# A masked row maximum taken head by head on VectorE, in a fused attention and token/channel mixer

## The chip, the cores and the metric

The kernel runs on one core of a Trainium2 chip. The metric is the device time of one execution in microseconds (us). TensorE is called PE in the profile (PEld are its weight loads), VectorE is DVE, ScalarE is ACT, GpSimd is POOL, and SyncE, which only issues DMAs here, is SP.

## The reference

Windowed attention over 8 batches, 8 heads, 576 positions of 64 values (the window is the position itself and the 63 before it), and behind it two mixers on the result x (576 tokens of 512 channels per batch):

```python
scores = scale * np.matmul(q, k.transpose(0, 1, 3, 2))
mask = (rel >= 0) & (rel < window)
scores = np.where(mask, scores, -1000000000.0)
scores = scores - np.max(scores, axis=-1, keepdims=True)
attn = np.exp(scores)
attn = attn / (np.sum(attn, axis=-1, keepdims=True) + 1e-09)
x = np.matmul(attn, v)                      # then heads side by side: B, S, H * D
xt = x.transpose(0, 2, 1)
h = np.maximum(xt @ w_tok1, 0.0) @ w_tok2   # token mixer, 576 -> 256 -> 576
u = x + h.transpose(0, 2, 1)
h2 = np.maximum(u @ w_ch1, 0.0) @ w_ch2     # channel mixer, 512 -> 1536 -> 512
return u + h2
```

The four mixer weights arrive as 64-bit floats. The kernel turns them into fp32 itself and splits each into a high and a low part, since each large product is made of three matmuls of rounded parts.

## The kernel before, in words

**Tiles.** The 72 blocks of 64 queries are done as 36 tiles, i = 0 to 35. A tile holds two query blocks on the 128 partitions and all 8 heads; its scores lie in two PSUM banks, `s[u]` with u = 0 and 1, four heads of 128 keys each. Nine tiles make a pair of batches (`TPP = 9`).

**One round of the loop.** For tile i the loop transposes the exponentials (`pt_transpose`, PE, then a copy by ACT), multiplies with v (`av`), scales by the reciprocal sums (`recip`, `norm`, on DVE) and splits x (ACT high part, POOL low part, `split_x`) for the token mixer. In the same round the softmax of tile i+1 runs: `softmax(i+1, u)` on DVE makes the masked scores and the negative row maximum `nm`, `softmax_exp` on ACT makes the exponentials head by head with their sums. At its end PE makes the scores of tile i+2 (`qk`). PE fills what is left with `tok1` (L387) and pieces of `tok2` (L428, L435).

**The mask.** For the first N_PE = 7 tiles PE adds the mask by a matmul (L287), and DVE takes the maximum straight from PSUM (L309) and scales it (L310). From tile 7 on, DVE does it in two instructions over all four heads of a bank: L312 reads the scores from PSUM, multiplies by the scale, adds the mask and writes `e` to SBUF; L315 reads `e` and takes the maximum of each head.

**The weights.** `job_load` loads a piece of 64-bit weights (`raw`), `job_convert_a` (L204, L206, L207) and `job_convert_b` (L216, L218, L219) convert it on DVE, POOL adds the halves (L221), and `job_finish` splits it (ACT high part; POOL or DVE low part). The table `JOBS` says in which rounds a conversion stands: one in rounds -1 to 5 and 12, and later in six of nine rounds.

**Order.** The order of the work on each engine is the order in which the code is written; nothing is rescheduled. All loads are issued by SP in that order. Round 0's loads are written out by hand ahead of the loop, those of the first batch's keys in five pieces.

**After the attention.** From 262 us on the kernel does the channel mixer, which PE fills almost alone; the change does not touch it.

Of the kernel before, what the change touches and what calls it, by code (L numbers as in the profile page):

```python
# [10 lines left out]
F32 = mybir.dt.float32  # L11
# [4 lines left out]
AF = mybir.ActivationFunctionType  # L16
ALU = mybir.AluOpType
AX = mybir.AxisListType
PSUM = bass.MemoryType.PSUM

B, H, S, D = 8, 8, 576, 64
C = H * D
P = 128
BLK = 64
NBLK = S // BLK
NPAIR = B // 2
TPP = 9
NT = NPAIR * TPP
# [11 lines left out]
N_FIRST = 28  # L40


JOBS = {i: 1 if i < 6 or i == 12 or i > 6 and i % TPP not in (0, 3, 5) else 0 for i in range(-1, 37)}
PIECES = {22: (1, 0), 23: (1, 0), 31: (1, 0), 32: (1, 0), 33: (1, 0), 34: (1, 0), 35: (3, 0), 36: (2, 1)}

TOK1_FROM, TOK1_SLOW, TOK2_FROM = 2, 4, 7
# [1 line left out]
N_PE, N_EARLY = 7, 4  # L48
# [9 lines left out]

HOME = {"m1": "c2", "m6": "c3", "m7": "c4", "m5": "c5", "m2": "c6", "m4": "c0", "m3": "c1"}
SLOT, NSLOT = NPROD * 2 * P, 3  # L60
NEG = -1.0e9

NEG_PE = -2.0 ** 33

F64_LOW = 2.0 ** -15
F64_HIGH = struct.unpack("<f", struct.pack("<I", 0x47EFFFFF))[0]
# [7 lines left out]
def tile_blocks(i):  # L74

    p, t = divmod(i, TPP)
    if t == 4:
        return (2 * p, 8), (2 * p + 1, 8)
    b, t = (2 * p, t) if t < 4 else (2 * p + 1, t - 5)
    return (b, t), (b, t + 4)  # L80
# [3 lines left out]
def mixer_kernel(ctx: ExitStack, tc: tile.TileContext, qh, kh, vh, wt1, wt2, wc1, wc2, out):  # L84
    nc = tc.nc
    scale = 1.0 / math.sqrt(D)
# [36 lines left out]
    with ExitStack() as actx:  # L123
        pa = actx.enter_context(tc.tile_pool(name="pa", bufs=1))
        qctx = ExitStack()
        pq = qctx.enter_context(tc.tile_pool(name="pq", bufs=1, side="right"))

        mask = [pa.tile([P, P], F32, name=f"mask{m}") for m in range(2)]

        kbs, loaded, cpool = {}, {}, [pq]  # L130

        def load_k(i):
            p, t = divmod(i, TPP)
            if t in (0, 4):
                b = 2 * p + (t == 4)
                kbs[b] = pq.tile([P, H // 2, (NBLK + 1) * BLK], F32, name=f"k{b}", tag="k", bufs=2)
                if b != 0:
                    nc.sync.dma_start(kbs[b], kh[b])

# [10 lines left out]
        maskr = [pa.tile([P, P], F32R, name=f"maskr{m}") for m in range(2)]  # L150
# [7 lines left out]
        def warm(k):  # L158
            for _ in range(k):
                nc.tensor.matmul(idle, zero[:, :P], zero, start=True, stop=True)  # L160
# [3 lines left out]
        for m in (1, 0):  # L164
            nc.gpsimd.memset(mask[m], 0.0)
            for half in range(2):
                mh = mask[m][half * BLK:(half + 1) * BLK]
                nc.gpsimd.affine_select(out=mh, in_=mh, compare_op=ALU.is_ge, fill=NEG,
                                        base=-1, pattern=[[1, P]], channel_multiplier=-1)
                nc.gpsimd.affine_select(out=mh, in_=mh, compare_op=ALU.is_ge, fill=NEG,  # L170
                                        base=BLK, pattern=[[-1, P]], channel_multiplier=1)
            if m == 1:
                nc.gpsimd.memset(mask[1][0:BLK, 0:BLK], NEG)
            nc.scalar.activation(maskr[m], mask[m], AF.Copy, scale=NEG_PE / NEG)

        for c in range(2):
            nc.gpsimd.tensor_copy(swapped[:, c * BLK:(c + 1) * BLK], ident[:, (1 - c) * BLK:(2 - c) * BLK])
# [53 lines left out]
        def job_load():  # L231
            if to_load:
                n = to_load.pop(0)
                src, _, _, o, m = jobs[n]
                raw = cpool[0].tile([P, CW], I64, name=f"raw{n}", tag="raw", bufs=3)
                nc.sync.dma_start(raw[:, :m], src[:, o:o + m])
                to_convert.append((n, raw))
# [3 lines left out]
        def job_convert_a():  # L241
            if to_convert:
                n, raw = to_convert.pop(0)
                to_convert_b.append((n, to_f32_a(raw, jobs[n][4], n, n >= N_FIRST)))

        def job_convert_b():
            if to_convert_b:
                n, part = to_convert_b.pop(0)
                to_finish.append((n, to_f32_b(*part)))
# [17 lines left out]
        s_ps, e_sb, st = {}, {}, {}  # L267

        def qk(i):

            qt, on_pe = loaded[i][0], i < N_PE
            s = []
            for u in range(2):

                if i == 1:
                    tag, bufs = "h", 2
                elif (i, u) == (N_PE, 1) or 2 <= i < N_PE and (2 * i + u) % 3 == 0:
                    tag, bufs = "up", 1
                else:
                    tag, bufs = "s", 2  # L280
                s.append(ps.tile([P, 4, P], F32, name=f"s{i}_{u}", tag=tag, bufs=bufs))
                s_ps[i, u] = s[u]
                if i == 0 and u == 0:
                    warm(4)
                if on_pe:
                    mk = maskr[1 if tile_blocks(i)[0][1] == 0 else 0]
                    nc.tensor.matmul(s[u], identr, mk.unsqueeze(1).to_broadcast([P, 4, P]), start=True, stop=False,  # L287
                                     skip_group_check=True)
            if i == 0:
                warm(3)  # L290
            for j in range(4):
                for u in range(2):
                    r = slice(u * BLK, (u + 1) * BLK)
                    for half, (b, n) in enumerate(tile_blocks(i)):
                        nc.tensor.matmul(s[u][half * BLK:(half + 1) * BLK, j], qt[r, j, half],
                                         kbs[b][r, j, n * BLK:n * BLK + P],
                                         start=not on_pe, stop=True, skip_group_check=on_pe)

        def softmax(i, u):
            if u == 0:  # L300
                st[i] = (pa.tile([P, H], F32, name=f"nm{i}", tag="nm", bufs=3),
                         pa.tile([P, H], F32, name=f"sum{i}", tag="sum", bufs=3))
            nm, sm = st[i]
            mk = mask[1 if tile_blocks(i)[0][1] == 0 else 0]
            e = pa.tile([P, 4, P], F32, name=f"e{i}_{u}", tag="e", bufs=4)
            e_sb[i, u] = e
            nmu = nm.rearrange("p (j u) -> p j u", u=2)[:, :, u]
            if i < N_PE:
                nc.vector.tensor_reduce(out=nmu, in_=s_ps[i, u], axis=AX.X, op=ALU.max, negate=True)  # L309
                nc.vector.tensor_scalar_mul(nmu, nmu, scale)  # L310
                return
            nc.vector.scalar_tensor_tensor(  # L312
                out=e, in0=s_ps.pop((i, u)), scalar=scale,
                in1=mk.unsqueeze(1).to_broadcast([P, 4, P]), op0=ALU.mult, op1=ALU.add)
            nc.vector.tensor_reduce(out=nmu, in_=e, axis=AX.X, op=ALU.max, negate=True)  # L315

        def softmax_exp(i, u):
            e = e_sb[i, u]
            nm, sm = st[i]
            src, by = (s_ps.pop((i, u)), scale) if i < N_PE else (e, 1.0)  # L320
            for h in range(4):
                g = 2 * h + u
                nc.scalar.activation(e[:, h], src[:, h], AF.Exp, bias=nm[:, g:g + 1], scale=by,  # L323
                                     accum_out=sm[:, g:g + 1])
# [22 lines left out]
        def recip(i):  # L347
            _, sm = st.pop(i)
            ri = pa.tile([P, H], F32, name=f"ri{i}", tag="ri", bufs=2)
            nc.vector.tensor_scalar_add(ri, sm, 1e-9)  # L350
            nc.vector.reciprocal(ri, ri)
            return ri

# [119 lines left out]
        def run_pieces(k):  # L473
            for _ in range(min(k, len(pieces))):
                tok2(*pieces.pop(0))

        load_k(0)
        load_q(0)
        k0, kh0 = (x[:, :, :8 * BLK].rearrange("p j (g n) -> p j g n", g=2) for x in (kbs[0], kh[0]))
        for g in range(2):  # L480
            nc.sync.dma_start(k0[:, :, g, :P], kh0[:, :, g, :P])
        load_q(1)
        for g in range(2):
            nc.sync.dma_start(k0[:, :, g, P:], kh0[:, :, g, P:])
        job_load()
        load_v(0)
        nc.sync.dma_start(kbs[0][:, :, 8 * BLK:], kh[0, :, :, 8 * BLK:])
        load_q(2)
        job_load()
        load_v(1)  # L490
        tok1_plan, n = {}, 0
        for i in range(TOK1_FROM, NT + 1):
            m = min(n + (1 if i < TOK1_SLOW else 2), i)
            tok1_plan[i] = range(n, m)
            n = m
        qk(0)
        for i in range(-1, NT + 1):
            if 0 <= i and i + 2 < NT:
# [5 lines left out]
            store_u()  # L504
            n_jobs = JOBS[i]
            if i == NT - 1:
# [8 lines left out]
                    pts.append(pt_transpose(i, 1))  # L515
            if i + 1 < NT:
                softmax(i + 1, 0)
            if early and i > 0:
                norm(*normed.pop())
            if 0 <= i < NT:  # L520
                ri = recip(i)
# [13 lines left out]
                    job_convert_a()  # L535
            if i == NT - 1:
                pts.append(pt_transpose(i, 1))
            if i + 1 < NT:
                softmax(i + 1, 1)
            if i < N_PE - 1:  # L540
                for _ in range(n_jobs):
# [38 lines left out]
    with ExitStack() as bctx:  # L580
# [105 lines left out]
        u = ul.pop(0)  # L686
# [12 lines left out]
        for ct in range(NCT):  # L699
# [3 lines left out]
            op = new_op("0", ct)  # L703
# [84 lines left out]
        for j in range(1, N_PLAIN):  # L788
            u, last = ul.pop(j), j == N_PLAIN - 1
# [4 lines left out]
            for half in range(2):  # L794
                g = []
# [33 lines left out]
                for ct in range(NCT):  # L829
                    op = new_op(f"{j}_{half}", ct)  # L830
# [141 lines left out]
```

## Time and profile before

| | |
|---|---|
| median of 3 runs | 842.85 us (841.65 to 843.45) |
| the profiled execution's own time | 843.08 us |
| its span, first to last instruction | 841.3 us |
| mean granted TensorE clock | 0.993 |
| PE busy in the span | 820.7 us |
| DVE, ACT, POOL busy in the span | 529.1, 336.6, 104.6 us |
| 57.30 to 249.88 us (tiles 6 to 34): DVE busy | 173.2 of 192.58 us |
| 262 to 841 us: PE busy | 574.2 of 579 us |

The time outside the span is 843.08 - 841.3 = 1.8 us. Rows of the timeline give start, duration, engine, line and operation, and in brackets the idle time ahead and what ended it. Rows on the same engine can overlap by some 0.08 us: the next instruction starts while the last one is leaving the pipeline, so costs are taken from start to start. A row of the chain of waits gives start, length and the work on the chain.

### The profile page before, as it was taken

Reading aid. Unit: us, or ns where it says so; the run is one execution under the profiler, and the core shown is the slowest. Engines: PE = TensorE matmul, PEld = TensorE weight load, DVE = VectorE, ACT = ScalarE, POOL = GpSimd, SP = SyncE. Lnnn points to the kernel's source line nnn. Section 1 sums busy time; section 2 is a strip of 40 time slices with the busy share of each in tenths; the row PEclk is TensorE's granted clock in tenths of the full one; section 3 lists DMA queues with packets and bytes.
Section 4 is the critical chain, followed back from the end, with each engine's and each line's share of the span. In section 5 each row is a group of like instructions: output and inputs, shape, how many; then the busy total and the mean of one; then the engine's idle time right before and its main releaser. Section 6 shows DMA issues by size and latency. Waiting matters only on the chain.

```text
span 841.3 us, 14830 instructions
## 1 busy us (share of the span) xinstructions
PE 820.7 (98%) x5878; PEld 681.4 (81%) x5878; DVE 529.1 (63%) x940; ACT 336.6 (40%) x1017; POOL 104.6 (12%) x110
## 2 busy tenths in 40 slices
PE   8989999999999999999999999999999999999998
PEld 5668888888879878888888888878888878888886
DVE  5889988888884795666425535367635367625252
ACT  6778889888885441213203211024202033202020
POOL 4433434343332000000000000000000000000000
PEclk9999999999999999999999999999999999999999
DMA  9657687677644546744413642324542424542002
GB/s 329 210 202 250 206 253 242 218 246 249 206 134 151 195 121 187 209 139 135 141 73 111 246 194 87 138 88 138 187 188 88 138 91 169 171 170 88 1 1 100
DMA packets 71621, 136.49 MB, mean 162 GB/s; under 512 B 7040, under 2 KB 41856, under 8 KB 69632
## 3 DMA queue, kind: packets, MB, share of 16 engines
q1 hardware_dynamic: 69440, 133.71, 46.8%
q10 hardware_dynamic: 2112, 1.84, 0.7%
q8 instruction: 46, 0.75, 0.4%
q14 instruction: 23, 0.19, 0.1%
HBM read 104.66 MB, written 30.87 MB: 161 GB/s over the span
## 4 chain that ended last, share of the span: by engine, by line
PE 69%; DVE 23%; issue 3%; ACT 3%; DMA 1%; SPq 0%; POOL 0%; POOLq 0%; DVEq 0%; ACTq 0%
PE gp L871 19%; PE op L659 11%; PE gp L651 8%; PE op_4a L659 4%; PE op_2b L659 4%; PE op_2a L659 4%; PE op_0b L659 4%; PE op_0a L659 4%; PE op_4b L659 4%; DVE nm L315 3%; DVE e L312 2%; PE up L435 2%; PE h L387 2%; DVE x L356 2%; DVE r L219 2%
## 5 line engine op out<-in xcount | busy, mean ns | idle before, releaser
L871 PE MATMUL gp<-m,w1hi 128*128 128x512 f32 x504 | 155.4, 389 | 0.7 <-DVE x L879 0.7
L871 PEld LDWEIGHTS gp<-m,w1hi 128*128 128x128 f32 x504 | 94.4, 188 | 21.2 <-DVE x L879 1.5
L871 PE MATMUL gp<-m,w1lo 128*128 128x512 f32 x252 | 98.1, 389 | 0.0
L323 ACT ACTIVATE e<-e,nm 128x128 f32<-128x128 f32 x232 | 90.5, 398 | 18.1 <-DVE nm L315 17.6
L638 ACT ACTIVATE ghi<-x 128x512 fp32r<-128x512 f32 x54 | 34.2, 632 | 119.9 <-DVE x L881 68.3
L875 ACT COPY x<-gp 128x512 f32<-128x512 f32 x18 | 10.4, 577 | 143.8 <-PE gp L871 143.8
L639 DVE SCALAR_TENSOR_TENSOR glo<-x,ghi 128x512 fp32r<-128x512 f32 x54 | 37.4, 693 | 38.1 <-ACT ghi L638 38.1
L638 ACT ACTIVATE ghi<-gp 128x512 fp32r<-128x512 f32 x50 | 29.8, 596 | 70.5 <-PE gp L651 70.4
L651 PE MATMUL gp<-ulo,w1hi 128*128 128x512 f32 x144 | 56.0, 389 | 0.0
L651 PE MATMUL gp<-uhi,w1hi 128*128 128x512 f32 x144 | 56.0, 389 | 0.0
L651 PE MATMUL gp<-uhi,w1lo 128*128 128x512 f32 x144 | 56.0, 389 | 0.0
L871 PEld LDWEIGHTS gp<-m,w1lo 128*128 128x128 f32 x252 | 47.3, 188 | 9.7
L342 PEld LDWEIGHTS xp<-v,pt 128*64 128x64 f32 x1152 | 38.2, 142 | 15.0 <-issue 7.0
L639 DVE SCALAR_TENSOR_TENSOR glo<-gp,ghi 128x512 fp32r<-128x512 f32 x50 | 34.4, 687 | 24.7 <-ACT ghi L638 24.6
L659 PE MATMUL op<-ghi,w2hi 128*128 128x512 f32 x128 | 49.8, 389 | 0.0
L659 PE MATMUL op<-ghi,w2lo 128*128 128x512 f32 x128 | 49.8, 389 | 0.0
L659 PE MATMUL op<-glo,w2hi 128*128 128x512 f32 x128 | 49.8, 389 | 0.0
L104 POOL TENSOR_TENSOR xlo<-x,xhi 128x512 fp32r<-128x512 f32 x32 | 41.3, 1290 | 40.3 <-ACT xhi L101 39.9
L342 PE MATMUL xp<-v,pt 128*64 128x64 f32 x1152 | 43.2, 230 | 2.1 <-ACT t1hi L101 1.9
L323 ACT ACTIVATION_READ_ACCUMULATOR e<-e,nm 128x1 f32 x232 | 45.0, 194 | 0.0
L435 PE MATMUL up<-t2hi,hhi 128*128 128x320 f32 (+1 forms) x128 | 43.0, 336 | 0.0
L330 PE MATMUL pp<-ident,e 128*128 128x128 f32 x288 | 42.2, 280 | 0.5
(168 smaller groups left out, 1888.4 us busy)
## 6 DMA issues: line engine op xcount, KB each, us to landing
v<-vh SPq DMA_DIRECT2D x36, 512.0 KB, 3.8
w1hi<-w1s SPq DMA_DIRECT2D x18, 896.0 KB, 4.5
w1lo<-w1s SPq DMA_DIRECT2D x18, 896.0 KB, 6.3
raw<-wc SPq DMA_DIRECT2D x32, 384.0 KB, 4.4
q<-qh SPq DMA_DIRECT2D x36, 256.0 KB, 4.4
k<-kh SPq DMA_DIRECT2D x7, 1280.0 KB, 8.3
out<-uf SPq DMA_DIRECT2D x35, 256.0 KB, 2.7
uf<-u_dram SPq DMA_DIRECT2D x8, 1024.0 KB, 9.1
```

What stands on the lines that cost most here:

```text
L104: eng_lo.tensor_sub(lo, src, hi.bitcast(F32))
L219: nc.vector.scalar_tensor_tensor(out=rf, in0=low.bitcast(U32), scalar=2.0 ** -52, in1=rf, op0=ALU.mult, op1=ALU.mult)
L315: nc.vector.tensor_reduce(out=nmu, in_=e, axis=AX.X, op=ALU.max, negate=True)
L323: nc.scalar.activation(e[:, h], src[:, h], AF.Exp, bias=nm[:, g:g + 1], scale=by, accum_out=sm[:, g:g + 1])
L330: nc.tensor.transpose(pp[:, h], e[:, h], ident)
L342: nc.tensor.matmul(xp[half * BLK:(half + 1) * BLK, h], pts[h % 2][:, h // 2, half * BLK:(half + 1) * BLK], vt[:, half, h], start=True, sto ...
L435: nc.tensor.matmul(up[:, :n], hx[:, cs], w[:, tt * S + s0:tt * S + s0 + n], start=False, stop=(k == 6), skip_group_check=True)
L638: nc.scalar.activation(hi, src, AF.Relu)
L639: nc.vector.scalar_tensor_tensor(out=lo, in0=src, scalar=0.0, in1=hi.bitcast(F32), op0=ALU.max, op1=ALU.subtract)
L651: nc.tensor.matmul(gp, w[:, w1_at(ft, ct)], x[:, ct], start=(k == 0), stop=(k == 3 * NCT - 1))
L659: nc.tensor.matmul(op, w[:, ct, ft], x[:, cols], start=(first and k == 0), stop=(last and k == 3 * len(gs) - 1), skip_group_check=not (fir ...
L871: nc.tensor.matmul(b, w[:, at], c[:, h, t], start=(n < 4 and k == 0), stop=(k == 5), skip_group_check=True)
```

## The change

**1. One DVE instruction per head for mask and maximum (tiles 7 to 35).** L312 and L315 go. For each of the four heads a `tensor_tensor_reduce` adds the mask to the scores, multiplies by minus the scale, writes `e`, and keeps the minimum, which is `nm`. The exponential then reads `e` with scale -1. The mask constant becomes -2^33 for all tiles, so that PE's copy of the mask is a plain cast.

**2. The first weight piece and the keys by another plan.** The first `raw` is loaded ahead of all else and converted ahead of the first softmax, and round -1 has no conversion any more. The keys are laid out block by block in place of head pair by head pair, so that the first batch's key pieces have runs of 2 KB in place of 512 bytes and come in 3 DMAs in place of 5. PE then reads the keys of a score matmul as two runs of 64.

**3. Round 0's second softmax half** stands right behind its first half.

**4. The sums plus 1e-9** are made by `scalar_tensor_tensor` with the sums as both tensors, (sum + 1e-9) max sum, in place of `tensor_scalar_add`.

```diff
-JOBS = {i: 1 if i < 6 or i == 12 or i > 6 and i % TPP not in (0, 3, 5) else 0 for i in range(-1, 37)}
+JOBS = {i: 1 if 0 <= i < 6 or i == 12 or i > 6 and i % TPP not in (0, 3, 5) else 0 for i in range(-1, 37)}
...
-                kbs[b] = pq.tile([P, H // 2, (NBLK + 1) * BLK], F32, name=f"k{b}", tag="k", bufs=2)
+                kbs[b] = pq.tile([P, NBLK + 1, H // 2, BLK], F32, name=f"k{b}", tag="k", bufs=2)
...
-            nc.scalar.activation(maskr[m], mask[m], AF.Copy, scale=NEG_PE / NEG)
+            nc.scalar.copy(maskr[m], mask[m])
...
-                        nc.tensor.matmul(s[u][half * BLK:(half + 1) * BLK, j], qt[r, j, half],
-                                         kbs[b][r, j, n * BLK:n * BLK + P],
+                        so = s[u][half * BLK:(half + 1) * BLK, j].rearrange("p (n c) -> p n c", n=2)
+                        nc.tensor.matmul(so, qt[r, j, half], kbs[b][r, n:n + 2, j],
...
-            nc.vector.scalar_tensor_tensor(
-                out=e, in0=s_ps.pop((i, u)), scalar=scale,
-                in1=mk.unsqueeze(1).to_broadcast([P, 4, P]), op0=ALU.mult, op1=ALU.add)
-            nc.vector.tensor_reduce(out=nmu, in_=e, axis=AX.X, op=ALU.max, negate=True)
+
+            s = s_ps.pop((i, u))
+            for h in range(4):
+                g = 2 * h + u
+                nc.vector.tensor_tensor_reduce(out=e[:, h], in0=s[:, h], in1=mk, scale=-scale, scalar=MAX_F32,
+                                               op0=ALU.add, op1=ALU.min, accum_out=nm[:, g:g + 1])
...
-            src, by = (s_ps.pop((i, u)), scale) if i < N_PE else (e, 1.0)
+            src, by = (s_ps.pop((i, u)), scale) if i < N_PE else (e, -1.0)
...
-            nc.vector.tensor_scalar_add(ri, sm, 1e-9)
+            nc.vector.scalar_tensor_tensor(out=ri, in0=sm, scalar=1e-9, in1=sm, op0=ALU.add, op1=ALU.max)
             nc.vector.reciprocal(ri, ri)
...
+        job_load()
         load_k(0)
         load_q(0)
-        k0, kh0 = (x[:, :, :8 * BLK].rearrange("p j (g n) -> p j g n", g=2) for x in (kbs[0], kh[0]))
-        for g in range(2):
-            nc.sync.dma_start(k0[:, :, g, :P], kh0[:, :, g, :P])
+        k0, kh0 = (x[:, :8].rearrange("p (g n) j c -> p g n (j c)", g=2) for x in (kbs[0], kh[0]))
+        nc.sync.dma_start(k0[:, :, :2], kh0[:, :, :2])
         load_q(1)
-        for g in range(2):
-            nc.sync.dma_start(k0[:, :, g, P:], kh0[:, :, g, P:])
-        job_load()
+        nc.sync.dma_start(k0[:, :, 2:], kh0[:, :, 2:])
         load_v(0)
-        nc.sync.dma_start(kbs[0][:, :, 8 * BLK:], kh[0, :, :, 8 * BLK:])
+        nc.sync.dma_start(kbs[0][:, 8:], kh[0, :, 8:])
...
+        job_convert_a()
+        job_convert_b()
         qk(0)
...
             if i + 1 < NT:
                 softmax(i + 1, 0)
+            if i == 0:
+                softmax(1, 1)
...
-            if i + 1 < NT:
+            if i + 1 < NT and i != 0:
                 softmax(i + 1, 1)
```

**How the orders move.** On SP, at the program's start, where `raw` are 64-bit weights, `q`, `k` and `v` the tiles' inputs, before:

```order
L142 DMA q_142<-qh 128x512
L481 DMA k_141<-kh 128x4x128 x2
L142 DMA q_146<-qh 128x512
L484 DMA k_141<-kh 128x4x128 x2
L236 DMA raw_150<-wt 128x320
L147 DMA v_152<-vh 128x1024
L487 DMA k_141<-kh 128x4x128
L142 DMA q_155<-qh 128x512
L236 DMA raw_157<-wt 128x320
```

On SP, the same place, now:

```order
L236 DMA raw_141<-wt 128x320
L142 DMA q_144<-qh 128x512
L483 DMA k_143<-kh 128x2x512
L142 DMA q_147<-qh 128x512
L485 DMA k_143<-kh 128x2x512
L147 DMA v_150<-vh 128x1024
L487 DMA k_143<-kh 128x512
L142 DMA q_153<-qh 128x512
L236 DMA raw_155<-wt 128x320
```

The first weight piece goes from behind the keys of tiles 0 to 3 to the front; the second one stays behind the same loads. On DVE, at the start, where `nm` is a tile's row maxima, before:

```order
L309 TENSOR_REDUCE nm_188<-s_0_161 128x4
L310 TENSOR_SCALAR nm_188<-nm_188 128x4
L309 TENSOR_REDUCE nm_188<-s_1_167 128x4
L310 TENSOR_SCALAR nm_188<-nm_188 128x4
L204 TENSOR_SCALAR c_200<-raw_150 128x320
L206 TENSOR_SCALAR c_200<-c_200 128x320
L207 TENSOR_SCALAR c_200<-c_200 128x320
L216 SCALAR_TENSOR_TENSOR c_200<-raw_150,c_200 128x320
L218 TENSOR_SCALAR r_208<-c_200 128x320
L219 SCALAR_TENSOR_TENSOR r_208<-raw_150,r_208 128x320
L309 TENSOR_REDUCE nm_256<-s_0_214 128x4
```

and now:

```order
L204 TENSOR_SCALAR c_159<-raw_141 128x320
L206 TENSOR_SCALAR c_159<-c_159 128x320
L207 TENSOR_SCALAR c_159<-c_159 128x320
L216 SCALAR_TENSOR_TENSOR c_159<-raw_141,c_159 128x320
L218 TENSOR_SCALAR r_163<-c_159 128x320
L219 SCALAR_TENSOR_TENSOR r_163<-raw_141,r_163 128x320
L309 TENSOR_REDUCE nm_196<-s_0_169 128x4
L310 TENSOR_SCALAR nm_196<-nm_196 128x4
L309 TENSOR_REDUCE nm_196<-s_1_175 128x4
L310 TENSOR_SCALAR nm_196<-nm_196 128x4
L309 TENSOR_REDUCE nm_256<-s_0_214 128x4
```

The first conversion stands ahead of the first two softmaxes in place of between them. On DVE, in the rounds from tile 7 on, from the second half of a round's softmax (`e_1`) to the next tile's first half (`e_0`), before:

```order
L312 SCALAR_TENSOR_TENSOR e_1_981<-s_1_915,mask_90 128x512
L315 TENSOR_REDUCE nm_954<-e_1_981 128x4
L216 SCALAR_TENSOR_TENSOR c_977<-raw_736,c_977 128x384
L218 TENSOR_SCALAR r_994<-c_977 128x384
L219 SCALAR_TENSOR_TENSOR r_994<-raw_736,r_994 128x384
L356 TENSOR_TENSOR x_1017<-xp_1000,ri_959 128x512
```

and now:

```order
L316 ISA e_1_985,nm_956<-s_1_917,mask_90 128x128
L316 ISA nm_956 128x1
L316 ISA e_1_985,nm_956<-s_1_917,mask_90 128x128
L316 ISA nm_956 128x1
L316 ISA e_1_985,nm_956<-s_1_917,mask_90 128x128
L316 ISA nm_956 128x1
L316 ISA e_1_985,nm_956<-s_1_917,mask_90 128x128
L316 ISA nm_956 128x1
L216 SCALAR_TENSOR_TENSOR c_981<-raw_734,c_981 128x384
L218 TENSOR_SCALAR r_1000<-c_981 128x384
L219 SCALAR_TENSOR_TENSOR r_1000<-raw_734,r_1000 128x384
L358 TENSOR_TENSOR x_1023<-xp_1006,ri_963 128x512
```

Two instructions become eight: each head has one over 128 elements and a second one that only writes the one value kept. The order of all the rest stays.

More of the change, by code (lines that the diff above doesn't have):

```diff
@@ L60 @@
 SLOT, NSLOT = NPROD * 2 * P, 3
-NEG = -1.0e9
-NEG_PE = -2.0 ** 33
+NEG = -2.0 ** 33
+MAX_F32 = 3.0e38
 F64_LOW = 2.0 ** -15
@@ L947 @@
     qh = qb[bi, ji].reshape(NT, 2, BLK, H // 2, 2, D).transpose(0, 4, 5, 3, 1, 2).reshape(NT, P, H // 2, 2, BLK)
-    kh = kb.reshape(B, NBLK + 1, BLK, H // 2, 2, D).transpose(0, 4, 5, 3, 1, 2).reshape(B, P, H // 2, (NBLK + 1) * BLK)
+    kh = kb.reshape(B, NBLK + 1, BLK, H // 2, 2, D).transpose(0, 4, 5, 1, 3, 2).reshape(B, P, NBLK + 1, H // 2, BLK)
     vw = np.stack([vb[bi, ji], vb[bi, ji + 1]], 2).reshape(NT, 2, P, H, D)
```

## The prediction

> **What bounds the kernel now.** I read the page's first part, then the windows by stage, the chain of waits of the attention stage, and last the timeline of DVE and POOL in one round.
>
> ```profile
> PE 820.7 (98%) x5878; PEld 681.4 (81%) x5878; DVE 529.1 (63%) x940; ACT 336.6 (40%) x1017; POOL 104.6 (12%) x110
> ...
> 57.30:249.88 192.58, 186.04 (x2616) 159.77 (x2615) 173.20 (x326) 164.22 (x618) 75.80 (x66) 1.00 0.68 224
> ...
> 262.00:841.00 579.00, 574.16 (x2568) 475.99 (x2566) 305.05 (x502) 127.97 (x233) 0.00 (x0) 1.00 0.39 134
> ```
>
> After the length, each window row gives the busy time of PE, PEld, DVE, ACT and POOL. From 262 us on PE is full and nothing of the change is there. In the 192.6 us of tiles 6 to 34 three engines are near full (PE 186, DVE 173, ACT 164), so the busy shares do not say which one sets the pace. The chain does. Its shares for the start (0 to 57.3 us, first row) and for 57.3 to 256 us (second):
>
> ```profile
> by line: DMA raw<-wt 9.7%; ACT e L323 9.5%; DVE nm L309 6.3%; issue 6.0%; DVE r L219 5.5%; DVE c L216 5.3%; DVE x L356 5.2%; PE h L387 4.8%; DVE nm L310 4.6%; DVE c L206 4.2%; DVE c L207 4.1%; DVE r L218 3.7%; PE xp L342 3.4%; ACT pt L332 3
> ...
> by line: DVE nm L315 11.7%; DVE e L312 10.5%; DVE x L356 6.9%; PE h L387 6.6%; DVE ri L350 6.4%; PE xp L342 6.1%; PE up L435 5.7%; DVE c L206 5.3%; DVE r L219 4.8%; issue 4.6%; DVE c L207 4.1%; DVE c L216 4.1%; DVE hlo L407 3.7%; DVE r L218
> ```
>
> In the second stretch (198.7 us) L315 has 11.7%, 23.2 us; at 686 ns each (next fence) that is 34 of its 58. So DVE sets the pace in 34 of 58 half softmaxes, PE in the rest.
>
> ```profile
> L315 DVE TENSOR_REDUCE nm<-e 128x4 f32<-128x512 f32 x57 | 39.1, 686 | 2.0
> L312 DVE SCALAR_TENSOR_TENSOR e<-s,mask 128x512 f32<-128x512 f32 x57 | 38.5, 676 | 1.6 <-PE s L295 1.6
> L350 DVE TENSOR_SCALAR ri<-sum 128x8 f32<-128x8 f32 x29 | 21.3, 735 | 0.0
> ```
>
> L350 adds 1e-9 to eight values per partition and takes 735 ns on average. One round shows why (DVE rows first, then POOL's):
>
> ```profile
> 190.80 0.56 DVE L219 SCALAR_TENSOR_TENSOR r<-raw,r 128x384 f32<-128x384 uint32 x1
> 191.28 0.68 DVE L356 TENSOR_TENSOR x<-xp,ri 128x512 f32<-128x512 f32 x1
> 191.88 0.68 DVE L312 SCALAR_TENSOR_TENSOR e<-s,mask 128x512 f32<-128x512 f32 x1
> 192.59 0.69 DVE L315 TENSOR_REDUCE nm<-e 128x4 f32<-128x512 f32 x1
> 193.20 0.80 DVE L350 TENSOR_SCALAR ri<-sum 128x8 f32<-128x8 f32 x1
> 194.03 0.20 DVE L351 RECIPROCAL ri<-ri 128x8 f32<-128x8 f32 x1
> 194.15 0.31 DVE L204 TENSOR_SCALAR c<-raw 128x384 int32<-128x384 int32 x1
> 194.50 1.08 DVE L206 TENSOR_SCALAR c<-c 128x384 f32<-128x384 f32 x1
> 195.89 0.68 DVE L312 SCALAR_TENSOR_TENSOR e<-s,mask 128x512 f32<-128x512 f32 x1
> ...
> 192.69 1.28 POOL L104 TENSOR_TENSOR xlo<-x,xhi 128x512 fp32r<-128x512 f32 x1 [0.25 <-ACT xhi L101]
> 194.35 1.01 POOL L104 TENSOR_TENSOR w1lo<-w,w1hi 128x384 fp32r<-128x384 f32 x1 [0.38 <-ACT w1hi L101]
> ```
>
> L350 starts at 193.20 and ends at 194.00, 0.03 after POOL's split of x (192.69 to 193.97). L206 does the same behind POOL's w1lo: 1.08, to 195.58, while POOL ends at 195.36. So these one-tensor instructions wait for POOL. L312, L315 and L356 keep their 0.68 in all rounds.
>
> **The change part by part.**
>
> *Start: weights, keys, round 0.* The loads land in the order of issue. q's first tile took 2.6 us from issue, the second key piece 4.2 (issued at 1.91, so 6.1), the second weight piece 6.9 (issued at 6.89, so 13.8):
>
> ```profile
> q<-qh SPq DMA_DIRECT2D x1, 256.0 KB, 2.6
> ...
> k<-kh SPq DMA_DIRECT2D x1, 256.0 KB, 4.2
> ...
> raw<-wt SPq DMA_DIRECT2D x1, 320.0 KB, 6.9
> ...
> 4.50 5.58 DMA raw<-wt
> ...
> 8.15 0.17 DVE L310 TENSOR_SCALAR nm<-nm 128x4 f32<-128x4 f32 x1
> 8.22 0.68 DVE L309 TENSOR_REDUCE nm<-s 128x4 f32<-128x512 f32 x1
> 10.10 0.33 DVE L204 TENSOR_SCALAR c<-raw 128x320 int32<-128x320 int32 x1 [0.99 <-DMA raw<-wt]
> 12.48 0.68 DVE L309 TENSOR_REDUCE nm<-s 128x4 f32<-128x512 f32 x1
> 14.89 0.31 DVE L204 TENSOR_SCALAR c<-raw 128x320 int32<-128x320 int32 x1
> 17.33 0.68 DVE L309 TENSOR_REDUCE nm<-s 128x4 f32<-128x512 f32 x1
> ```
>
> A conversion takes 2.4 us (10.10 to 12.48; 14.89 to 17.33). In first place the first piece lands at about 0.74 + 2.6 + 0.3 for 320 in place of 256 KB, near 4 us, and is converted by 6.4, while DVE has nothing else: its first softmax starts at 7.42 before. Tile 0's scores then need 320 KB more ahead of them, at the 0.25 to 0.35 MB per us of these landings up to 1.0 us; the two key pieces' longer runs may give that back. So softmax 0 ends between 9.1 and 10.1 and tile 1's two halves (1.6 us) by 11.7. The second weight piece still has the same loads and bytes ahead of it: 13.8 at the latest, some 12.8 if the keys run at q's pace. Its conversion ends at 15.2 to 16.2, and tile 2's softmax starts there in place of 17.33: 1.1 to 2.1 earlier. The start's chain behind the first landing is DVE, ACT, POOL and PE without a load, so the shift is handed on. I take **-1.7 us**; bounds -2.1 and, if late keys use it all up, +0.5. SP queues nothing new: one DMA moved, two fewer.
>
> *Mask and maximum.* Before, a half costs 0.71 (L312 at 191.88 to L315 at 192.59) plus 0.61 (to 193.20), 1.32 us. Now it is four pairs. A DVE instruction over 512 elements takes 0.60 from start to start (191.28 to 191.88), one over 384 takes 0.48 (190.80 to 191.28), so by that slope one over 128 takes 0.22 to 0.24. The row that writes the kept value has no twin on DVE. Its low end is L310 on four values, 0.07 (8.15 to 8.22), for a pair of 0.29 and a half of 1.16. For the high end ScalarE has such pairs:
>
> ```profile
> 191.11 0.39 ACT L323 ACTIVATE e<-e,nm 128x128 f32<-128x128 f32 x1
> 191.40 0.19 ACT L323 ACTIVATION_READ_ACCUMULATOR e<-e,nm 128x1 f32 x1
> ...
> 192.52 0.36 ACT L440 COPY u<-up 128x256 f32<-128x256 f32 x1
> 192.78 1.08 ACT L332 COPY pt<-pp 128x512 f32<-128x512 f32 x2
> ```
>
> There the 128-element instruction holds its engine 0.29, longer than a plain copy of 256 elements (0.26), so the read waits for its result; with 0.12 for that on DVE (L312 to L315 is 0.11 over the 0.60) the pair is 0.41 and the half 1.64. No wait stands between the two instructions in the order, which speaks for the low end; I take 0.32, so 1.28 and -0.04 per half. Of the 34 halves on the chain some 13 are first halves followed by a waiting L350 (12.7 us of it on the chain), which takes up the difference either way; 21 count. 21 x -0.04 = **-0.8 us**; bounds 21 x -0.16 = -3.4 and 21 x 0.32 = +6.7.
>
> [...]
>
> The score bank is free only after the fourth head, 1.28 us in place of 0.68. At the end of a round PE's L295 waits for the second bank, and av, tok2 pieces and transposes are queued behind it. I cost it at nothing: PE stands idle later in such rounds anyway, waiting for ACT's copy of u. Without that cover it is 0.6 us a round. ACT gets the first head's maximum some 1 us earlier, but then waits for x (L356) all the same.
>
> *Sums.* No two-SBUF-tensor instruction ran beside POOL in this trace, so the wait's fate is unknown. Even without a wait the next one-tensor instruction takes it over, as where L350 slipped in ahead of POOL (178.78 to 180.08):
>
> ```profile
> 178.72 0.16 DVE L350 TENSOR_SCALAR ri<-sum 128x8 f32<-128x8 f32 x1
> 179.03 1.26 DVE L204 TENSOR_SCALAR c<-raw 128x384 int32<-128x384 int32 x1
> 178.78 1.30 POOL L104 TENSOR_TENSOR xlo<-x,xhi 128x512 fp32r<-128x512 f32 x1 [3.36 <-ACT xhi L101]
> ```
>
> In rounds with a conversion (two of three) only L350's own 0.16 and L351's 0.12 would go. I take **0**; bounds 0 and -6 (9 such waits on the chain at 0.3, and 3 full ones near 1.1 in rounds without a conversion).
>
> [...]
>
> *Keys as two runs of 64, mask cast:* nothing. 1152 score matmuls of 128 columns keep PE busy 41.9 us, as many av matmuls of 64 columns 43.2: the columns do not set their pace.
>
> ```profile
> L342 PE MATMUL xp<-v,pt 128*64 128x64 f32 x1152 | 43.2, 230 | 2.1 <-ACT t1hi L101 1.9
> ...
> L295 PE MATMUL s<-k,q 64*64 64x128 f32 x1152 | 41.9, 282 | 0.2 <-DMA k<-kh 0.2
> ```
>
> **Sum:** 843.1 - 1.7 - 0.8 = 840.6 for the profiled execution, which lies 0.2 above the median of the runs: **840 us**.
>
> **The rivals.**
>
> *Slower: the kept value is read only once the pass has drained.* Place: the four pairs of every second half. It decides from a pair of 0.36 us on, where 21 x (4 x 0.36 - 1.32) = 2.5 eats the start's gain. For it: ScalarE does it. Against: no wait in the order. At 0.41 the sum is 843 - 1.7 + 6.7 = 848. If even the read's 0.16 is paid alone (0.53 a pair, +0.8 a half) first halves outlast POOL too: 34 x 0.8 less 13 x 0.65 of L350's waiting is +19, 860.
>
> *Faster: the two-tensor sums do not wait for POOL.* 840 - 6 = 834; with pairs of 0.29, 831. For it: none of L350's cousins with two tensors is ever long; against: none met POOL.
>
> *Nothing to see: the start's gain is eaten* by later keys or by the next waits for POOL (L310 and L206 at 20 to 35 us), and the pairs cost what they replace: 842.5.
>
> **How the numbers follow.** Forecast 0.42 (its own range 837 to 842), faster rival 0.20, no difference 0.13, slower rival 0.25. A difference of 0.2% (1.7 us) is about what a measurement can tell from none; some 0.07 of the forecast lies within it. Faster 0.35 + 0.20 = 0.55, same 0.20, slower 0.25. The range reaches down to the faster rival with cheap pairs, 829, and up to a pair of 0.45, 852; its far end at 860 stays outside.
>
> **What would show it.** Start: L204 first at about 4 us, tile 2's first L309 between 15.2 and 16.2. Pairs: start of one to start of the next 0.32, in 0.29 to 0.41. Sums: L352's mean near 0.7 if it waits, 0.16 if not, and then a longer L204 or L206. The granted clock and everything behind 262 us stay. The prediction is wrong if a pair takes over 0.36, if L295 waits for DVE for more than 0.2 us a round, or if tile 2's softmax starts no earlier.

## The result, and the profile after

The changed kernel takes 832.07 us (median of 4 runs, 831.61 to 832.63), the kernel before 843.15 us beside it: a ratio of 0.987, 95% interval 0.9858 to 0.9881, or 11 us less. The profiled execution has a span of 830.5 us. The forecast was 840 with a range of 829 to 852: the sign is right and the time is inside the range, but it lies below the forecast's own range of 837 to 842, and the gain is nearly four times the forecast one.

First the page's busy times and its chain of the whole span, after:

```profile
PE 814.5 (98%) x5878; PEld 678.9 (82%) x5878; DVE 508.6 (61%) x1288; ACT 336.4 (41%) x1017; POOL 104.8 (13%) x110
...
PE 83%; DVE 9%; ACT 4%; issue 2%; DMA 1%; POOLq 0%; POOL 0%; DVEq 0%; ACTq 0%; SPq 0%
```

DVE's part of the chain was 23% before. The stages are cut where the av matmuls of tiles 6 and 34 begin (57.30 and 249.88 us before). After, the windows of the start and of tiles 6 to 34 (length, then busy time of PE, PEld, DVE, ACT, POOL, and the granted clock), and the chain of waits of the second one:

```profile
0.00:55.15 55.15, 45.07 (x570) 32.77 (x571) 42.45 (x111) 38.90 (x154) 24.22 (x40) 1.00 0.74 265
55.15:238.98 183.83, 183.44 (x2616) 159.43 (x2615) 153.37 (x658) 163.19 (x615) 75.92 (x66) 1.00 0.71 235
```

```profile
by line: PE h L389 19.8%; PE up L437 19.3%; PE xp L344 14.7%; PE s L296 14.1%; PE pp L332 11.5%; PE up L430 8.5%; ACT e L325 5.0%; ACT hhi L400 1.6%; ACT pt L334 1.2%; ACT u L442 0.9%; issue 0.9%; DVE e L316 0.6%; DVE ri L352 0.6%; ACT w1hi
```

The start lost 2.15 us (57.30 to 55.15), tiles 6 to 34 lost 8.75 (192.58 to 183.83); the rest, 591.5 us, is as long as before. In tiles 6 to 34 PE is now busy for 183.44 of 183.83 us. DVE, which had L312, L315 and L350 for 28.6% of that chain, has next to nothing there (L316 and L352, 0.6% each).

The groups of DVE in that window, after (busy, mean ns of one, idle time before it):

```profile
L316 DVE CUSTOM_DVE_ANT_0 e<-s,mask 128x128 f32<-128x128 f32 x223 | 51.0, 285 | 4.1 <-PE s L296 3.7
L352 DVE SCALAR_TENSOR_TENSOR ri<-sum 128x8 f32<-128x8 f32 x28 | 26.5, 946 | 0.0
L316 DVE DVE_READ_ACCUMULATOR2_ANT nm<- 128x1 f32 x222 | 18.5, 83 | 0.0
```

These busy times hide what a pair costs, because its two rows overlap the rows beside them. The timeline of one round shows it (DVE and POOL):

```profile
176.54 0.29 DVE L316 CUSTOM_DVE_ANT_0 e<-s,mask 128x128 f32<-128x128 f32 x1 [0.28 <-PE s L296]
176.76 0.08 DVE L316 DVE_READ_ACCUMULATOR2_ANT nm<- 128x1 f32 x1
176.76 0.29 DVE L316 CUSTOM_DVE_ANT_0 e<-s,mask 128x128 f32<-128x128 f32 x1
176.97 0.08 DVE L316 DVE_READ_ACCUMULATOR2_ANT nm<- 128x1 f32 x1
...
176.99 1.28 POOL L104 TENSOR_TENSOR xlo<-x,xhi 128x512 fp32r<-128x512 f32 x1 [0.25 <-ACT xhi L101]
...
177.39 0.90 DVE L352 SCALAR_TENSOR_TENSOR ri<-sum 128x8 f32<-128x8 f32 x1
178.33 0.20 DVE L353 RECIPROCAL ri<-ri 128x8 f32<-128x8 f32 x1
...
179.69 1.02 POOL L104 TENSOR_TENSOR w1lo<-w,w1hi 128x384 fp32r<-128x384 f32 x1 [1.41 <-ACT w1hi L101]
...
180.10 0.29 DVE L316 CUSTOM_DVE_ANT_0 e<-s,mask 128x128 f32<-128x128 f32 x1
180.31 0.08 DVE L316 DVE_READ_ACCUMULATOR2_ANT nm<- 128x1 f32 x1
180.31 0.81 DVE L216 SCALAR_TENSOR_TENSOR c<-raw,c 128x384 int32<-128x384 int32 x1
```

Three things are to be read here. A pass starts 0.21 us after the one before it (176.76, 176.97), and the row that reads the kept value starts in the same instant as the next pass: it takes no time of its own. So a half is 4 x 0.21 = 0.84 us in place of 1.32. L352 ends at 178.29, 0.02 after POOL's split (176.99 + 1.28): the sums still wait for POOL, and by coming 0.48 us earlier they wait longer, 946 ns in the mean where L350 took 735. And the passes themselves, which read the scores from PSUM and one tensor from SBUF, run at 0.21 us in the middle of POOL's instruction (180.10 to 180.31), while L216 behind them, with two tensors in SBUF, takes 0.81 us in place of 0.56.

### The profile page after: what moved, and what is told of

It reads as the page before. It is cut to its first block, busy times and chain, and to the rows that moved or that the text cites. A ratio compares the mean times of both kernels' runs of the same rounds, so it can differ in the third digit from the quotient of the medians.

```text
span 830.5 us, 15190 instructions
## 1 busy us (share of the span) xinstructions
PE 814.5 (98%) x5878; PEld 678.9 (82%) x5878; DVE 508.6 (61%) x1288; ACT 336.4 (41%) x1017; POOL 104.8 (13%) x110
## 4 chain that ended last, share of the span: by engine, by line
PE 83%; DVE 9%; ACT 4%; issue 2%; DMA 1%; POOLq 0%; POOL 0%; DVEq 0%; ACTq 0%; SPq 0%
PE gp L876 19%; PE op L664 11%; PE gp L656 8%; PE up L437 5%; PE h L389 5%; PE op_2a L664 4%; PE op_4a L664 4%; PE op_0a L664 4%; PE op_0b L664 4%; PE op_2b L664 4%; PE op_4b L664 4%; PE xp L344 3%; PE s L296 3%; PE pp L332 3%; PE up L430 2%; ACT e L325 2%
## 5 line engine op out<-in xcount | busy, mean ns | idle before, releaser
L316 DVE CUSTOM_DVE_ANT_0 e<-s,mask 128x128 f32<-128x128 f32 x232 | 53.0, 285 | 4.1 <-PE s L296 3.7
L344 PE MATMUL xp<-v,pt 128*64 128x64 f32 x1152 | 41.5, 225 | 1.0 <-ACT pt L334 0.6
```

The source lines that it names most:

```text
L316: nc.vector.tensor_tensor_reduce(out=e[:, h], in0=s[:, h], in1=mk, scale=-scale, scalar=MAX_F32, op0=ALU.add, op1=ALU.min, accum_out=nm[:, ...
L344: nc.tensor.matmul(xp[half * BLK:(half + 1) * BLK, h], pts[h % 2][:, h // 2, half * BLK:(half + 1) * BLK], vt[:, half, h], start=True, sto ...
```

## Experiments

**Which part brought what.** Two kernels split the change. The first is the kernel before with part 1 alone:

```diff
-            nc.vector.scalar_tensor_tensor(
-                out=e, in0=s_ps.pop((i, u)), scalar=scale,
-                in1=mk.unsqueeze(1).to_broadcast([P, 4, P]), op0=ALU.mult, op1=ALU.add)
-            nc.vector.tensor_reduce(out=nmu, in_=e, axis=AX.X, op=ALU.max, negate=True)
+            s = s_ps.pop((i, u))
+            for h in range(4):
+                g = 2 * h + u
+                nc.vector.tensor_tensor_reduce(out=e[:, h], in0=s[:, h], in1=mk, scale=-scale, scalar=MAX_F32,
+                                               op0=ALU.add, op1=ALU.min, accum_out=nm[:, g:g + 1])
```

> The kernel before with part 1 alone (one pass per head, mask constant and exponential's scale with it). Theory D (VectorE's time in the masked halves of tiles 7 to 35 was the price; a half went from 1.32 to 0.84 us): the whole steady gain, -8.7 us, and none of the start's: 843.2 - 8.7 = 834.4 us (833.7 to 835.2). Rival S (the sums or the keys' layout brought part of what the trace shows between tiles 6 and 34): less than -7, so above 836. Tile 6's av starts at 57.3 us as before.

Measured: 834.29 us (833.42 to 834.67), ratio 0.9895, interval 0.988 to 0.9909. The second is the changed kernel with those lines the other way round:

> The changed kernel with part 1 undone: the pass with mask and the maximum over four heads as two instructions again (mask constant -2^33, which the pass adds to the scaled scores). Theory D: only the start's gain stays, 843.2 - 2.1 = 841.0 us (840.3 to 841.8), tiles 6 to 34 take 192.6 us again. Rival S: part of the steady gain stays, 836 to 840.

Measured: 840.29 us (839.96 to 841.07), ratio 0.9969, interval 0.9958 to 0.9981. The window of tiles 6 to 34, first with part 1 alone, then without it:

```profile
57.60:241.41 183.81, 183.43 (x2615) 159.43 (x2614) 153.41 (x656) 163.22 (x615) 75.99 (x66) 1.00 0.70 235
```

```profile
55.04:247.62 192.58, 186.03 (x2616) 159.79 (x2615) 173.22 (x326) 164.28 (x618) 75.82 (x66) 1.00 0.67 224
```

183.81 and 192.58 us are, to 0.02 us, the lengths after and before. So the whole 8.75 us between tiles 6 and 34 are the pass per head; sums and key layout have no share in it. The start's 2.1 us (by the traces) to 2.6 us (by the times) come with the other parts. Rival S is out.

**Is it DVE's time, and at what rate?** More passes are put behind the four, into a scrap tile, so that ScalarE still gets each maximum as early (the second kernel has `range(4)`):

```diff
+            for h in range(2):
+                pd = pa.tile([P, P], F32, name=f"pd{i}_{u}_{h}", tag="pd", bufs=1)
+                nc.vector.tensor_tensor_reduce(out=pd, in0=s[:, h], in1=mk, scale=-scale, scalar=MAX_F32,
+                                               op0=ALU.add, op1=ALU.min, accum_out=pn[:, h:h + 1])
```

> The changed kernel with two more passes per half behind the four, into a scrap tile (six pairs of 0.21 = 1.26 us a half, what four pairs of 0.315 would take; ScalarE still gets each head's maximum as early). Theory D, with the prediction's 21 halves that count: 843.2 - 2.1 + 21 x (1.26 - 1.32) = 839.8 us (838.5 to 842). Rival A (ScalarE's earlier start with the first head is the gain, not VectorE's time): below 834.

> The changed kernel with four more passes per half into a scrap tile (eight pairs, 1.68 us a half, what four pairs of 0.42 would take). Theory D: 843.2 - 2.1 + 21 x (1.68 - 1.32) = 848.7 us, and up to 853 if first halves outlast GpSimd's split too (34 halves in place of 21). Rival A: below 836.

Measured: 841.85 us (841.32 to 843.78; ratio 0.9991, 0.9981 to 1.0) with two, 859.65 us (859.48 to 860.64; ratio 1.0201, 1.0184 to 1.0218) with four. The first is 2 us above the expected 839.8, though inside its range; the second is above its whole range. The timeline of the first gives one reason (the second extra pass, the half's first pass, and what follows the half):

```profile
151.34 0.08 DVE L321 DVE_READ_ACCUMULATOR2_ANT pn<- 128x1 f32 x1
151.46 0.29 DVE L321 CUSTOM_DVE_ANT_0 pd<-s,mask 128x128 f32<-128x128 f32 x1
...
154.35 0.28 DVE L317 CUSTOM_DVE_ANT_0 e<-s,mask 128x128 f32<-128x128 f32 x1
...
155.74 0.55 DVE L216 SCALAR_TENSOR_TENSOR c<-raw,c 128x384 int32<-128x384 int32 x1
```

With one scrap tile the second extra pass overwrites the first one's output and starts 0.12 us late. A half is 1.39 us (154.35 to 155.74), and 2.06 with four. The last run repeats the first with a scrap tile for each pass:

```diff
-                pd = pa.tile([P, P], F32, name=f"pd{i}_{u}_{h}", tag="pd", bufs=1)
+                pd = pa.tile([P, P], F32, name=f"pd{i}_{u}_{h}", tag="pd", bufs=2)
```

> The kernel with two more passes per half, now into two scrap tiles in place of one. With one tile the second pass waited 0.12 us for the first one's write (151.34 to 151.46 in the trace), so that a half took 1.39 us, not 1.26. Theory D: a half of 1.26 us, just under the prediction's 1.28; with its 21 halves 843.2 - 2.1 + 21 x (1.26 - 1.32) = 839.8 us (838.8 to 841), 2 to 2.5 below the kernel with one scrap tile (841.9), which by the same sum should be at 843.2 - 2.1 + 21 x 0.07 = 842.6. Rival (some other cost of the extra passes, such as the score bank's later release, made up its 9.8 us): no difference between the two, 841.9.

Measured: 839.21 us (838.75 to 841.06; ratio 0.9958, 0.9942 to 0.9975), 2.6 us below the kernel with one scrap tile. The windows of tiles 6 to 34 of the three, in the order two passes with a tile each, two with one tile, four with one tile:

```profile
56.50:247.72 191.22, 188.09 (x2615) 160.67 (x2614) 172.98 (x886) 162.89 (x615) 75.53 (x66) 1.00 0.67 226
```

```profile
56.63:250.25 193.62, 188.80 (x2616) 160.95 (x2615) 174.44 (x888) 162.72 (x615) 75.95 (x66) 1.00 0.67 223
```

```profile
54.19:265.40 211.21, 193.96 (x2615) 162.58 (x2614) 195.66 (x1112) 162.30 (x615) 75.86 (x66) 1.00 0.61 204
```

| a half softmax takes | tiles 6 to 34 | us per us of a half, from the row above |
|---|---|---|
| 0.84 (the change) | 183.83 | |
| 1.27 | 191.22 | 17 |
| 1.32 (before; all four maxima come at the end) | 192.58 | 27 |
| 1.39 | 193.62 | 15 |
| 2.06 | 211.21 | 26 |

From 1.27 to 1.39 it is 2.40 / 0.12 = 20 us per us. This is not DVE's time alone, though: the extra passes also read the score bank, so that it comes free later, and PE's score matmuls wait for it. In the same order of kernels (us in total, times, longest):

```profile
PE s L297 <- DVE pn L321: 1.1, 3, 0.4
```

```profile
PE s L297 <- DVE pn L321: 2.7, 7, 0.5
```

```profile
PE s L297 <- DVE pn L321: 13.3, 15, 1.2
```

Before the change and after it PE has no such wait. So up to 1.6 of the 2.40 us, and up to 10.6 of the 17.59 us from 1.39 to 2.06, can be the bank, and the slopes are no clean count of the halves that wait for DVE. With two passes and a tile each the bank can explain at most 1.1 of the 7.39 us lost against the change; the rest follows the time added on DVE. Rival A is out: with ScalarE's early maximum kept, most of the gain goes when DVE's time comes back.

**Does the read of the kept value cost anything?** Four plain additions of one head's scores and the mask, of the same size and without a kept value, stand in place of the four extra passes:

```diff
-                nc.vector.tensor_tensor_reduce(out=pd, in0=s[:, h], in1=mk, scale=-scale, scalar=MAX_F32,
-                                               op0=ALU.add, op1=ALU.min, accum_out=pn[:, h:h + 1])
+                nc.vector.tensor_add(pd, s[:, h], mk)
```

> The changed kernel with four plain additions per half (scores of one head plus mask, 128x128, no kept value) behind the four passes. It prices the row that reads the kept value. Theory F (the read costs nothing): a plain addition takes 0.21 us from start to start, as a pass with its read does, and the time is that of the kernel with four more passes, 859.7 +- 1.5 us. Rival: the read holds the engine, a plain addition takes 0.13 to 0.16 us from start to start, and the time is 850 to 855 us.

One run: 858.29 us. The timeline (the four additions in one row, then the sums):

```profile
151.23 1.26 DVE L320 TENSOR_TENSOR pd<-s,mask 128x128 f32<-128x128 f32 x4
152.41 0.16 DVE L355 SCALAR_TENSOR_TENSOR ri<-sum 128x8 f32<-128x8 f32 x1
```

Four additions take 1.18 us from start to start. If the three that follow a write to the same scrap tile wait 0.12 for it, as the extra passes did, it is (1.18 - 3 x 0.12) / 4 = 0.21 us each, as much as a pass with its read. So the read costs nothing from start to start.

**The sums.** The first kernel puts the one-tensor form back into the changed kernel:

```diff
-            nc.vector.scalar_tensor_tensor(out=ri, in0=sm, scalar=1e-9, in1=sm, op0=ALU.add, op1=ALU.max)
+            nc.vector.tensor_scalar_add(ri, sm, 1e-9)
```

> The changed kernel with part 4 undone: the sums plus 1e-9 by tensor_scalar_add again. Theory W (the instruction with two tensors in SBUF waits for GpSimd as the one with a single tensor does; in the trace after it takes 0.93 us on average): no difference from the changed kernel, 832.1 us (831.4 to 832.8), and a mean of the add in 0.85 to 1.0 us between tiles 6 and 34. Rival: the two forms differ by where they wait, more than 1 us either way.

Measured: 831.48 us (831.28 to 832.32), ratio 0.9863, interval 0.9847 to 0.988, which overlaps that of the changed kernel. Its group from 57.3 to 250 us:

```profile
L352 DVE TENSOR_SCALAR ri<-sum 128x8 f32<-128x8 f32 x29 | 27.1, 936 | 0.0
```

936 against 946 ns: the two forms wait alike, and part 4 does nothing. Beside POOL, L352 and L216, with two tensors in SBUF, were seen to wait (946 ns in the mean; 0.81 us in place of 0.56), as was the addition with one (936 ns); L316, with one in PSUM and one in SBUF, was not (0.21 us). What decides this is not shown.

What the wait was worth is shown by leaving the addition out, in the kernel before and in the changed one. The reciprocal then reads the sums (the edit of the kernel before is shown):

```diff
-            nc.vector.tensor_scalar_add(ri, sm, 1e-9)
-            nc.vector.reciprocal(ri, ri)
+            nc.vector.reciprocal(ri, sm)
```

> The kernel before without the addition of 1e-9. It prices the prediction's faster rival: if the reciprocal does not wait for GpSimd, the waits of 12.7 us on the chain go, and what the next instruction with one tensor takes over decides: -6 us (837) if rounds without a conversion and the excess over 0.16 us count, 0 to -2 (841 to 843) if the reciprocal or the conversion behind it takes over the wait.

Measured: 835.35 us (834.49 to 836.23), ratio 0.9907, interval 0.9892 to 0.9922: 8 us less, more than the 6 of the faster rival. Its window of tiles 6 to 34, its group of L204 there, and two rounds of its timeline, with a conversion behind the sums and without:

```profile
55.82:241.39 185.57, 183.80 (x2615) 159.39 (x2615) 157.19 (x298) 164.96 (x618) 76.12 (x66) 1.00 0.69 232
```

```profile
L204 DVE TENSOR_SCALAR c<-raw 128x384 int32<-128x384 int32 x20 | 15.7, 786 | 0.0
```

```profile
185.88 1.28 POOL L104 TENSOR_TENSOR xlo<-x,xhi 128x512 fp32r<-128x512 f32 x1 [0.24 <-ACT xhi L101]
186.38 0.19 DVE L350 RECIPROCAL ri<-sum 128x8 f32<-128x8 f32 x1
186.50 0.88 DVE L204 TENSOR_SCALAR c<-raw 128x384 int32<-128x384 int32 x1
...
192.35 1.28 POOL L104 TENSOR_TENSOR xlo<-x,xhi 128x512 fp32r<-128x512 f32 x1 [0.26 <-ACT xhi L101]
192.85 0.19 DVE L350 RECIPROCAL ri<-sum 128x8 f32<-128x8 f32 x1
192.96 0.64 DVE L312 SCALAR_TENSOR_TENSOR e<-s,mask 128x512 f32<-128x512 f32 x1
```

The reciprocal does not wait for POOL, and neither does the masking pass behind it. Where a conversion follows, L204 takes the wait over, but only what is left of it: 0.88 - 0.31 = 0.57 us here; its mean is 786 ns. So 7 of the 8 us are from tiles 6 to 34 (192.58 to 185.57).

> The changed kernel without the addition of 1e-9: the reciprocal reads the sums themselves (a sum holds exp(0) = 1, so in fp32 the 1e-9 is lost in any case). Theory P (from tile 6 on TensorE is the bound now, VectorE's waits there cost nothing): 0 to -0.8 us, all of it ahead of tile 6: 831.3 to 832.1; tiles 6 to 34 stay at 183.8 us. Rival: the waits for GpSimd, 27 us of VectorE's time, still cost: 829.5 or less. If the reciprocal itself waits for GpSimd, its own mean shows it (0.9 us in place of 0.2).

Measured, in the changed kernel: 831.62 us (830.56 to 833.7), ratio 0.9866, interval 0.9848 to 0.9883, no different from it. Its window:

```profile
54.04:237.49 183.45, 183.07 (x2616) 159.47 (x2615) 142.54 (x632) 163.02 (x615) 75.28 (x66) 1.00 0.69 235
```

DVE has 10.8 us less to do there and the stage is 0.38 us shorter. The two gains, 8.75 and 7.01 us, do not add up, since either brings PE to within 2 us of full.

**The start.** Part 3 is undone in the changed kernel:

```diff
-            if i == 0:
-                softmax(1, 1)
...
-            if i + 1 < NT and i != 0:
+            if i + 1 < NT:
                 softmax(i + 1, 1)
```

> The changed kernel with part 3 undone: round 0's second softmax half stands behind the conversion again. Theory E (most of the start's 2.1 us is the earlier first piece, part 2): 832.1 to 832.9 us, and tile 2's first maximum within 0.6 us of its place in the changed kernel. Rival: the start's gain hangs on part 3, since tile 1's exponentials wait for that half: 833.5 or more, tile 6's av at 56.5 us or later.

Measured: 832.51 us (831.38 to 833.34), ratio 0.9872, interval 0.9858 to 0.9887: no difference that can be told from none. Tile 2's first maximum starts at 16.17 us, in the changed kernel at 16.18. Parts 3 and 4 bring nothing that shows, so part 2 is left for the start's gain. Its pieces (the early weights, the keys' layout, the fewer DMAs) were not tried one by one, and some of this gain goes together with the granted clock (last section).

**A faster version?** With the pass at 0.21 us, tiles 2 to 6 could use it too, in place of PE's mask matmul, the maximum from PSUM and the scaling, which runs beside POOL in seven of these ten halves and takes up to 1173 ns there in place of 170 (L310 of the changed kernel). The changed kernel without the 1e-9, and with this (4 in the second kernel; N_MASK also replaces N_PE in `qk` and `softmax_exp`):

```diff
+N_MASK = 2
...
-            if i < N_PE:
+            if i < N_MASK:
                 nc.vector.tensor_reduce(out=nmu, in_=s_ps[i, u], axis=AX.X, op=ALU.max, negate=True)
```

> The changed kernel without the addition of 1e-9 and with the pass per head from tile 2 on in place of 7 (TensorE's mask matmul, the maximum from PSUM and the scaling go for tiles 2 to 6). Theory H (GpSimd blocks the conversions that come next, and in tiles 3 to 6 ScalarE and the weights' chain set the end): 0 to -1 us against the same kernel from tile 7 on (831.6): 830.6 to 831.8. Rival: the ten halves give 0.1 to 0.6 us each, since the waiting scaling of four values is on the chain of the start: 827 to 830 us.

> The same from tile 4 on: between the two, 830.8 to 831.8 us by theory H; by the rival 829 to 830.5.

Measured: 830.86 us (830.42 to 833.56; ratio 0.986, 0.9844 to 0.9877) and 830.93 us (830.35 to 832.1; ratio 0.9865, 0.985 to 0.9879). Both intervals overlap the changed kernel's. The times are those of theory H: the ten halves bring under 1 us. Its reason was not tested by a run of its own. No version here is shown to be faster than the change.

## Why the prediction was right and wrong

**What bounds the kernel: right.** DVE set the pace in part of the halves: 8.75 us for 0.48 us less a half are worth 18 halves, near the 21 that were counted. Nothing moved behind 262 us.

**Mask and maximum: the term that was mis-sized.** It stood at -0.8 us with bounds of -3.4 and +6.7; it is -8.75. The step that failed is the price of the pair: "I take 0.32", from a low end of 0.29 that added 0.07 for the read to 0.22 for the pass. Measured are 0.21 for both: the read starts together with the next pass. With that price the prediction's own sum gives 21 x (4 x 0.21 - 1.32) = -10.1 us; 1.3 of it do not show, with PE busy for all but 0.4 us by then. The row taken for the read, L310 on four values, was that of an instruction that reads a tile; nothing in the trace before showed that the read costs anything, and the low end should have been a pair of 0.22, -9.2 us. The order had pointed there (no wait between the two), and 0.22 for 128 elements had been worked out from the slope. Where 0.32 was nearly put to the test, in the kernel with a half of 1.27 us, the time is 839.2 against the forecast's 840.

**Start: the steps right, half of the size from elsewhere.** Forecast -1.7 with a bound of -2.1; the trace shows -2.15 and the kernel without part 1 -2.6. The steps, after:

```profile
3.72 0.36 DVE L204 TENSOR_SCALAR c<-raw 128x320 int32<-128x320 int32 x1 [2.60 <-DMA raw<-wt]
8.80 0.69 DVE L309 TENSOR_REDUCE nm<-s 128x4 f32<-128x512 f32 x1 [2.50 <-PE s L296]
13.06 0.28 DVE L204 TENSOR_SCALAR c<-raw 128x320 int32<-128x320 int32 x1
16.18 0.69 DVE L309 TENSOR_REDUCE nm<-s 128x4 f32<-128x512 f32 x1 [0.63 <-PE s L296]
...
22.47 0.68 DVE L309 TENSOR_REDUCE nm<-s 128x4 f32<-128x512 f32 x1
...
26.47 0.33 DVE L206 TENSOR_SCALAR c<-c 128x320 f32<-128x320 f32 x1
```

The first conversion starts at 3.72 us (forecast about 4) and tile 2's softmax at 16.18 (forecast 15.2 to 16.2, 17.33 before). That is 1.15 us, the low end; it waits 0.63 us there for PE's scores, which the forecast did not have on the path. The other microsecond was not in the sum. Before:

```profile
19.07 1.98 PE L342 MATMUL xp<-v,pt 128*64 128x64 f32 x32 [1.88 <-ACT t1hi L101]
22.13 1.99 PE L295 MATMUL s<-k,q 64*64 64x128 f32 x32
24.15 0.69 DVE L309 TENSOR_REDUCE nm<-s 128x4 f32<-128x512 f32 x1 [0.67 <-PE s L295]
...
27.69 1.28 DVE L206 TENSOR_SCALAR c<-c 128x320 f32<-128x320 f32 x1
```

PE's granted clock was 0.50 there from 20 to 24 us (last section), so that 32 score matmuls took 1.99 us (1.10 after) and tile 3's softmax waited 0.67 for them; it now starts 1.68 us earlier (24.15 to 22.47). At L206 the lead is 1.22 us again (27.69 to 26.47), and 2.17 at its end: there L206 ran beside POOL (27.35 to 28.78 us) and took 1.28 us, now it takes 0.33.

**Sums: the number right, its reason only in part.** The term is 0 because the sums wait as before. The forecast had left that open and took 0 because the next instruction would take the wait over; that, and the bound of -6 for a wait that goes, were wrong: without the instruction the kernel before gains 8 us. "The next one-tensor instruction takes it over" holds for only a part of each wait, and not at all in rounds without a conversion.

**Costs put at nothing.** The bank's later release costs nothing that shows: PE stands idle for 0.4 us in 183.8. Keys as two runs of 64 cost nothing: the score matmuls from 57 to 250 us, before and after, take 275 and 276 ns.

```profile
L295 PE MATMUL s<-k,q 64*64 64x128 f32 x896 | 31.3, 275 | 0.0
```

```profile
L296 PE MATMUL s<-k,q 64*64 64x128 f32 x878 | 30.4, 276 | 0.0
```

**The rivals.** The slower one needed a read that waits for its pass; it does not. The faster one had nearly the time that came (834, 831 with cheap pairs), but its mechanism is false here: the sums wait. The stated range reached 829 only by this rival, so that 832 lies inside it is luck; what the forecast's own terms allowed ended at 837. The pair's 0.21 also lies outside the 0.29 to 0.41 that were to show it. "Nothing to see" fell with the pair.

## What to carry to other kernels

Price an instruction that no trace shows from start to start, and let the low end of its second half be nothing when no wait stands before it: on DVE a pass that keeps a value per row cost 0.21 us for 128 columns, read included, so one pass over the data beat two even at four times the instructions (0.84 against 1.32 us a half). Before adding up gains, ask which engine is next: here either of two fixes brought PE close to its full share, and the second was then worth hardly anything (0.38 us of the stage). The sums, made to come 0.48 us earlier here, only waited longer for POOL (946 ns in place of 735); what helped was to remove them (7 us in the kernel before), and their other form, with one tensor, waited alike (936 ns).

## What the runs showed of the hardware that was not expected

**The granted clock at the start.** The forecast said that the clock stays. From 16 to 28 us it was 0.72 before and 1.00 after (the number ahead of the last two), and in the kernel with two extra passes, whose start is that of the changed kernel, 0.79 from 12 to 20 us:

```profile
16.00:28.00 12.00, 10.06 (x117) 7.62 (x116) 10.70 (x25) 8.78 (x37) 5.29 (x6) 0.72 0.87 343
```

```profile
16.00:28.00 12.00, 10.03 (x165) 7.59 (x158) 11.17 (x25) 10.32 (x44) 5.72 (x6) 1.00 0.91 342
```

```profile
12.00:20.00 8.00, 7.18 (x104) 5.44 (x104) 4.98 (x15) 6.26 (x26) 1.12 (x2) 0.79 1.02 410
```

All three profiles with the old start show such a dip between 16 and 28 us (from 20 to 24 us 0.50 in the kernel before and in the one with part 1 alone, 0.75 in the kernel before without the 1e-9); in the first two PE has paused for 1.88 us ahead of it. Of the eleven with the new start three show one, between 12 and 20 us (from 12 to 16 us 0.66 with the pass from tile 2 on, 0.69 and 0.72 with two passes more, in two tiles and in one); from 4 to 12 us PE is idle there for less than 0.1 us. In the latter two av of tile 6 starts at 56.50 and 56.63 us; without such a dip it starts at 55.15 in the changed kernel, at 54.04 in that without the 1e-9, at 54.19 with four passes more and at 55.04 with part 1 undone. So such a dip goes with a start some 2 us longer. A second dip, between 44 and 57 us (0.87 to 0.90), stands in eleven of the fourteen profiles and goes with no longer start: of the four without the first one, the changed kernel alone lacks it, and its 55.15 is the latest of them. With it (the kernel before) and without it (the changed kernel) PE has paused alike, for 2.29 and 2.27 us, to 47.62 and 45.45 us.

What makes a dip come in one execution and not in another was not tried, so it is open whether the new start avoids the first one or was lucky. One run of the kernel before had a granted clock of 1.000, and its 841.3 us were the fastest of all its runs; the run at 1.000 of the kernel without part 1 took 840.8. With the clock alike the start's gain may thus be smaller than 2 us. The lead of 1.15 us at tile 2 also goes with the full clock: in the kernels with two extra passes, whose profiles have the dip, that softmax starts at 17.65 and 17.52 us, no earlier than the 17.33 before.

**The reciprocal.** On eight values per partition it passes POOL's instruction unhindered (0.19 us at 192.85, with POOL from 192.35 to 193.63), where an addition on the same values waits.
